# Seven half-size products for token blocks 2 and 3 in the first MLP's first matmul (slices 2 to 7)

## The chip, the core and the metric

The program runs on one core of one Trainium2 chip. The metric is device time in microseconds (us) of one execution; the number to be predicted is the median of several executions of the changed kernel. Five engines work side by side, each through its own queue in order: TensorE (PE, matmuls, with weight loads PEld that overlap them), VectorE (DVE), ScalarE (ACT), GpSimd (POOL) and SyncE (SP, which issues the transfers from HBM). Semaphores tie the queues together. A wait holds up everything that stands behind it in the same queue.

## The reference

The operator is a linear attention, a dense MLP and a domain-weighted MLP, one after the other, over 2304 tokens of width 512:

```python
def _attn_ref(q, k, v, g_norm):
    kv = np.einsum('bhsd,bhse->bhde', k, v)
    out = np.einsum('bhsd,bhde->bhse', q, kv)
    rms = np.sqrt(np.mean(out * out, axis=-1, keepdims=True) + 1e-06)
    return (out / rms * g_norm).astype(np.float32)

def _moe_ref(x, w_in, w_out):            # x 2304 x 512, w_in 512 x 2048, w_out 2048 x 512
    h = np.maximum(x @ w_in, 0.0)
    return (h * h @ w_out).astype(np.float32)

def _moe2_ref(x, domain_probs, w1, w2):  # four domains, w1 512 x 1024, w2 1024 x 512 each
    p = domain_probs / (domain_probs.sum(-1, keepdims=True) + 1e-09)
    for e in range(4):
        h = np.maximum(x @ w1[e], 0.0)
        out += p[:, e:e + 1] * (h @ w2[e])
    return out
```

The weights of the first MLP, w_in and w_out, arrive as float64; all other inputs are float32.

## The kernel before

**Numbers in two halves.** Every matmul operand is held as a high part and a low part (`split`: ACT copies the rounded high part, POOL subtracts it from the full value to get the low part). A product is three matmuls, low times high, high times low and high times high, so a 128-deep step of a product costs three matmuls of up to 512 columns.

**Tiles.** The tokens stand in five blocks (`BLK`): blocks 0 to 3 of 512 tokens, block 4 of 256. The hidden dimension of an MLP is cut into slices of 256. The first MLP has slices 0 to 7; the second MLP has 16 slices and is run in two groups, blocks 0, 1 and 4 first (slices 8 to 23 of the program), then blocks 2 and 3 (slices 24 to 39).

**Units.** The order of the work is a list of short names, each a call of one function:

- `f v.j.c` (`g1`): first product of slice v, block j, hidden half c: 4 depth steps of 3 matmuls, 12 in all, then in the first MLP ACT takes the relu, squares it and copies the high part `hh`, and POOL makes the low part `hl`.
- `g v.j.c` (`g2a`): second product of the first MLP for one 128-wide piece of the output, 6 matmuls; DVE adds the result from PSUM into the accumulator `acc`.
- `s v.b.i` (`g1s`), for i from 0 to 6: the first product of two blocks together in the second MLP, by seven products of half depth (6 matmuls of 512 columns each) in place of eight. The four PSUM banks are called pa, pb, pc and pd. Between the products run an ACT copy p1 and five DVE additions, u2, u4, and then the results of pb, pc and pd in place. Products 4, 5 and 6 add into banks pc, pa and pd that were written before, so product 4 waits for u4 to have read pc, product 5 for p1 to have read pa, and product 6 for the addition that makes pb to have read pd.
- `h` (`g2b`): second product of the second MLP. `x` (`right`): makes the sums of token blocks that `s` needs, when a group begins.
- `w` (`split_w`) takes the next 512-wide piece of weights and calls for a later one. In the first MLP a slice has four pieces, two of w_in and two of w_out; `w` starts `narrow`, five DVE operations and one ACT operation that turn float64 into two float32, and `y` (`split_narrowed`) splits the oldest narrowed piece, one operation on ACT and two on POOL. In the second MLP `w` works on pieces of two, and `operands` makes the sums of quarter tiles of the weights (four DVE operations) that `s` needs.

**Order.** `RAMP` is an order written out by hand for attention and slices 0 and 1; `rest()` makes the order after that. For slices 2 to 7 it runs over the blocks 0, 1, 2, 3, 4: first product of one block (`f` twice), second product of the block before (`g` four times), then a `y` and a `w` for the weights of a later slice. The instructions of each engine come out nearly in that order, shifted where a scheduler saw a wait. The short-lived tiles come from one pool, `tmp`, with eight places; a ninth waits until one is given back.

Of the kernel before, what the change touches and what calls it, by code (L numbers as in the profile page):

```python
# [120 lines left out]
def fused_kernel(ctx, tc, kvm, kvt, qt, g2, probs, w64, w32, out):  # L121
# [112 lines left out]

    def operands(i, v):
        r = raw.pop(i).rearrange("p c (k f) -> p (c k) f", k=2)
        w_t[v] = [
            wp.tile([P, 2, 4, 2, P], F32R, tag="a", name=f"a{v}"),  # L240
            ext.tile([P, 2, 4, 2, P], F32R, tag="a2", name=f"a2_{v}", bufs=2),
        ]
# [396 lines left out]
```

## Time and profile before

| | us |
|---|---|
| median of 3 runs | 1216.82 (1216.55 to 1217.67) |
| the profiled execution, its own time | 1214.15 |
| its span in the trace | 1212.4 |

The profiled execution is 2.67 us under the median and lies 1.75 us over its own span. Busy times of an engine are shares of the span. The matmuls of the trace overlap each other (one of 512 columns shows 390 ns, but the next begins earlier), so a rate per matmul is to be taken from a run of matmuls without a gap, not from the mean of one.

### The profile page before, as it was taken

How to read it: one execution, taken by the hardware profiler on the slowest of the kernel's cores; microseconds unless marked ns; L12 is line 12 of the kernel's file. 1: busy time of each engine (PE TensorE's matmuls, PEld its weight loads, DVE VectorE, ACT ScalarE, POOL GpSimd, SP SyncE). 2: the span in 40 equal slices, each digit the busy share in tenths (PEclk: the TensorE clock that was granted, in tenths of full speed). 3: DMA queues.
4: the chain of work that ended last, by engine and by line, in shares of the span. 5: the costliest groups of instructions: out<-in, count | busy, mean ns of one | idle time of the engine just before them, and what ended most of it. 6: DMA issues, size and time to landing. Idle time of an engine off the chain costs nothing.

```text
span 1212.4 us, 14974 instructions
## 1 busy us (share of the span) xinstructions
PE 1193.0 (98%) x5768; PEld 1003.2 (83%) x5768; DVE 765.8 (63%) x1177; ACT 439.9 (36%) x798; POOL 500.3 (41%) x390
## 2 busy tenths in 40 slices
PE   7999999999999999999999999999999999999998
PEld 6888788888888888888888888888788888888887
DVE  5968845545546466566666566656876666666655
ACT  4575444434445563222222222322433232323220
POOL 3556635445546675222323222323645242434310
PEclk9999999999999999999999999999999999999999
DMA  8611201111111101110111101111131121111101
GB/s 317 233 42 53 88 18 53 35 36 53 44 44 45 59 20 33 37 36 35 36 53 35 52 35 35 36 52 35 52 123 70 35 70 35 67 38 63 42 1 70
DMA packets 22247, 70.20 MB, mean 58 GB/s; under 512 B 2720, under 2 KB 2720, under 8 KB 22176
## 3 DMA queue, kind: packets, MB, share of 16 engines
q1 hardware_dynamic: 21888, 69.22, 16.7%
q8 instruction: 45, 0.74, 0.2%
q14 instruction: 26, 0.21, 0.1%
q10 hardware_dynamic: 288, 0.04, 0.0%
HBM read 64.52 MB, written 4.72 MB: 57 GB/s over the span
## 4 chain that ended last, share of the span: by engine, by line
PE 91%; DVE 5%; DMA 1%; issue 1%; POOL 1%; ACT 1%; SPq 0%; DVEq 0%; POOLq 0%; ACTq 0%
PE p L529 32%; PE p L377 18%; PE p L398 15%; PE pa L484 7%; PE pd L484 7%; PE pc L484 7%; PE pb L484 4%; PE po L301 1%; DVE u L179 1%; DMA kvs<-in_kvm 1%; DVE u L182 1%; DVE k L188 1%; DMA raw<-in_w 1%; DVE u L175 0%; PE pt L344 0%
## 5 line engine op out<-in xcount | busy, mean ns | idle before, releaser
L529 PE MATMUL p<-b,hh 128*128 128x512 f32 x1152 | 382.8, 390 | 0.5 <-ACT hh L516 0.5
L529 PEld LDWEIGHTS p<-b,hh 128*128 128x128 f32 x1152 | 216.3, 188 | 45.0 <-ACT hh L516 0.7
L539 DVE SCALAR_TENSOR_TENSOR acc<-p,p_sb,acc 128x512 f32<-128x512 f32 x270 | 199.4, 745 | 49.7 <-PE p L529 49.1
L529 PE MATMUL p<-b,hl 128*128 128x512 f32 x576 | 224.6, 390 | 0.0
L377 PE MATMUL p<-x,a 128*128 128x512 f32 (+1 forms) x960 | 204.3, 368 | 0.0
L377 PEld LDWEIGHTS p<-x,a 128*128 128x128 f32 x960 | 167.7, 189 | 30.4 <-PE po L301 0.2
L398 PE MATMUL p<-hh,b 128*128 128x512 f32 (+1 forms) x640 | 189.7, 370 | 0.0
L149 POOL TENSOR_TENSOR a<-raw,a 128x512 fp32r<-128x512 f32 x64 | 85.6, 1338 | 232.8 <-DVE pd L511 149.0
L405 DVE TENSOR_TENSOR acc<-p,acc 128x512 f32<-128x512 f32 (+1 forms) x140 | 87.9, 633 | 142.6 <-PE p L398 141.7
L149 POOL TENSOR_TENSOR b<-raw,b 128x512 fp32r<-128x512 f32 x64 | 82.1, 1303 | 188.0 <-ACT b L148 186.7
L149 POOL TENSOR_TENSOR hl<-s,hh 128x512 fp32r<-128x512 f32 (+1 forms) x80 | 97.9, 1226 | 120.0 <-ACT hh L148 116.7
L398 PEld LDWEIGHTS p<-hh,b 128*128 128x128 f32 x640 | 116.5, 189 | 20.2 <-ACT hh L148 0.4
L529 PEld LDWEIGHTS p<-b,hl 128*128 128x128 f32 x576 | 108.2, 188 | 21.4 <-DVE hl L517 0.2
L398 PE MATMUL p<-hl,b 128*128 128x512 f32 (+1 forms) x320 | 118.3, 370 | 2.4 <-POOL hl L149 2.4
L484 PE MATMUL pc<-o,a 128*128 128x512 f32 x384 | 97.6, 390 | 2.1 <-DVE u L499 2.1
L484 PE MATMUL pa<-o,a 128*128 128x512 f32 x384 | 97.6, 389 | 0.0
L484 PE MATMUL pd<-o,a 128*128 128x512 f32 x384 | 97.4, 389 | 0.0
L149 POOL TENSOR_TENSOR a<-w,a 128x512 fp32r<-128x512 f32 x64 | 85.0, 1328 | 25.3 <-ACT a L148 25.3
L148 ACT ACTIVATE a<-raw 128x512 fp32r<-128x512 f32 x64 | 40.1, 629 | 140.6 <-DMA raw<-in_w 109.2
L382 ACT ACTIVATE r<-p 128x512 f32<-128x512 f32 (+1 forms) x80 | 44.1, 552 | 122.2 <-PE p L377 121.7
L484 PEld LDWEIGHTS pc<-o,a 128*128 128x128 f32 x384 | 72.0, 188 | 17.5 <-DVE u L499 2.5
L484 PEld LDWEIGHTS pd<-o,a 128*128 128x128 f32 x384 | 72.1, 188 | 15.0
(92 smaller groups left out, 1477.3 us busy)
## 6 DMA issues: line engine op xcount, KB each, us to landing
raw<-in_w SPq DMA_DIRECT2D x96, 512.0 KB, 3.7
kvm<-in_kvm SPq DMA_DIRECT2D x10, 512.0 KB, 4.0
q<-in_qt SPq DMA_DIRECT2D x18, 256.0 KB, 4.6
out<-acc SPq DMA_DIRECT2D x18, 256.0 KB, 3.5
kvs<-in_kvm SPq DMA_DIRECT2D x6, 512.0 KB, 7.2
kvt<-in_kvt SPq DMA_DIRECT2D x4, 256.0 KB, 6.0
p_raw<-in_probs ACTq DMA_DIRECT2D x1, 36.0 KB, 4.8
g_sb<-in_g ACTq DMA_DIRECT2D x1, 0.5 KB, 4.3
```

The source lines that it names most:

```text
L148: nc.scalar.activation(out=hi, in_=full, func=AF.Copy)
L149: nc.gpsimd.tensor_tensor(out=lo, in0=full, in1=hi.bitcast(F32), op=ALU.subtract)
L179: nc.vector.scalar_tensor_tensor(out=u, in0=high, scalar=0xC0000000, in1=u, op0=ALU.bitwise_and, op1=ALU.bitwise_or)
L182: nc.vector.scalar_tensor_tensor(out=u.bitcast(F32), in0=k, scalar=1.125 * 2.0**-15, in1=u.bitcast(F32), op0=ALU.is_ge, op1=ALU.mult,)
L188: nc.vector.scalar_tensor_tensor(out=k.bitcast(F32), in0=low, scalar=2.0**-52, in1=k.bitcast(F32), op0=ALU.mult, op1=ALU.mult)
L377: nc.tensor.matmul(pt[:, :n], w, x, start=(i == 0), stop=(i == len(steps) - 1))
L382: nc.scalar.activation(out=r[:, :n], in_=pt[:, :n], func=AF.Relu)
L398: nc.tensor.matmul(pt[:, :n], w, h, start=(i == 0), stop=(i == len(steps) - 1))
L405: nc.vector.tensor_tensor(out=a, in0=pt[:, :n], in1=a, op=ALU.add)
L484: nc.tensor.matmul(pr[bank], x, y, start=(m == 0 and not more), stop=(m == len(steps) - 1), skip_group_check=more,)
L529: nc.tensor.matmul(pt, h, w, start=(i == 0), stop=(i == len(steps) - 1))
L539: nc.vector.scalar_tensor_tensor(out=a, in0=pt, scalar=pe, in1=a, op0=ALU.mult, op1=ALU.add)
```

## The change

In slices 2 to 7 the first product of blocks 2 and 3 is no longer four `f` units but seven `s` units, as the second MLP has them. Blocks 0, 1 and 4 stay as they are. Around it:

- The right operands (the sums t1 to t4 of the token blocks) are made once, in slice 2, by the new `right_first` (`e0` to `e3`). It writes t1, t2 and t3 into a new tile `e`, and t4 over a part of block 3's tile.
- The left operands are made for each slice: `left_parts` splits the pieces of w_in in halves of 256 columns into two tiles, a and a2, and `left_sums` adds the quarter tiles when the next `w` comes. For this `y` adds the two halves of a narrowed piece of w_in on POOL first.
- The order of the blocks in a slice is 0, 1, 4, then 2 and 3 (in slice 7: 0, 1, 2 and 3, then 4). `w` and `y` stand at other places, and `RAMP` has one `w` less, so the weights run one piece closer to their use.
- Weight tiles have two places, not three; in the second MLP a third place lies in the pool `ext`. `ext` now opens after the first MLP, so the tiles `hh` and `hl` have two places in slices 2 to 7, not three.
- `g1` squares in place of writing a second short-lived tile.

```diff
-g1.0.2 y w g0.4.3 g1.0.3 y f1.1.0 f1.1.1 f1.2.0 f1.2.1 w y w g1.1.0 g1.1.1 y g1.1.2 g1.2.0
+g1.0.2 y w g0.4.3 g1.0.3 y f1.1.0 f1.1.1 f1.2.0 f1.2.1 w y g1.1.0 g1.1.1 y g1.1.2 g1.2.0
...
-    for v in range(2, NS1):
-        for j in range(NB):
-            r += [f"f{v}.{j}.{fc}" for fc in range(FC)] + second(*prev)
-            r += ["y"] * (j > 0)
-            if j < (4, 4, 4, 4, 4, 2)[v - 2]:
-                r += ["w"]
-            prev = (v, (j,))
-            if v == NS1 - 1 and j >= 2:
-                r += [f"x0.{j - 2}"]
+    for v in range(FROM, NS1):
+        last = v == NS1 - 1
+        for n, blk in enumerate(((0,), (1,), (2, 3), (4,)) if last else ((0,), (1,), (4,), (2, 3))):
+            b = blk[0]
+            if len(blk) == 1:
+                r += [f"f{v}.{b}.{fc}" for fc in range(FC)] + second(*prev)
+                r += [f"e{n}"] if v == FROM and n < 2 else []
+                r += ["y", "w"] if n < 2 else ["y"]
+            else:
+                if v == FROM:
+                    r += ["e2", "e3"]
+                units = [f"s{v}.{b}.{i}" for i in range(7)]
+                for at, u in ((7, "x0.1"), (7, "x0.2"), (5, "x0.0")) if last else ((3, "w"),):
+                    units.insert(at, u)
+                r += merge(units[:3], second(*prev)) + units[3:] + ["y"] + ["w"] * (not last)
+            prev = (v, blk)
...
-    wp = ctx.enter_context(tc.tile_pool(name="wp", bufs=3))
+    wp = ctx.enter_context(tc.tile_pool(name="wp", bufs=2))
...
     def split_w():
+        if len(parts) == 2:
+            left_sums(parts[0][0], *(full for _, full in parts))
+            parts.clear()
...
     def split_narrowed():
         if narrowed:
-            hi, lo, top, rest = narrowed.pop(0)
+            v, c, hi, lo, top, rest = narrowed.pop(0)
+            if v >= FROM and c < 2:
+                nc.gpsimd.tensor_tensor(out=top, in0=top, in1=rest, op=ALU.add)
+                left_parts(v, c, top.rearrange("p (k f) -> p k f", k=2))
+                return
...
+    def left_parts(v, c, full):
+        for n, a in enumerate(w_t[v][:2]):
+            a = a.rearrange("p x k (h f) -> p x (k h) f", h=2)
+            split(a[:, 0, 2 * c : 2 * c + 2, :], a[:, 1, 2 * c : 2 * c + 2, :], full[:, :, n * P : (n + 1) * P])
+        parts.append((v, full))
...
+    def left_sums(v, first, other):
+        a11, a21, a12, a22 = (r[:, :, f : f + P] for r in (first, other) for f in (0, P))
+        st = [tmp.tile([P, 2, 2, P], F32, tag="tmp", name=f"w{n}_{v}") for n in range(2)]
+        s1, s2, s3, s4 = (st[n][:, m] for n in range(2) for m in range(2))
         nc.vector.tensor_tensor(out=s1, in0=a21, in1=a22, op=ALU.add)
         nc.vector.tensor_tensor(out=s2, in0=s1, in1=a11, op=ALU.subtract)
         nc.vector.tensor_tensor(out=s3, in0=a11, in1=a21, op=ALU.subtract)
         nc.vector.tensor_tensor(out=s4, in0=a12, in1=s2, op=ALU.subtract)
+        for n in range(2):
+            a = w_t[v][n].rearrange("p x k (h f) -> p x (k h) f", h=2)
+            split(a[:, 0, 4:8, :], a[:, 1, 4:8, :], st[n].rearrange("p m k f -> p (m k) f"))
...
+    def right_first(i):
+        if i == 0:
+            e = early.tile([P, 2, 6, 512], F32R, name="e")
...
+        for k in range(2):
+            full = tmp.tile([P, 512], F32, tag="tmp", name=f"{name}_{k}")
+            if name in ("t1", "t3"):
+                p, m = ("b12", "b11") if name == "t1" else ("b22", "b12")
+                low = tmp.tile([P, 512], F32, tag="tmp", name=f"{name}l_{k}")
+                nc.gpsimd.tensor_tensor(out=low, in0=half(p, k, 1), in1=half(m, k, 1), op=ALU.subtract)
+                nc.vector.tensor_tensor(out=full, in0=half(p, k, 0), in1=half(m, k, 0), op=ALU.subtract)
+            else:
+                p, m = ("b22", "t1") if name == "t2" else ("b21", "t2")
+                nc.vector.tensor_tensor(out=full, in0=half(p, k, 0), in1=t_tmp[m, k], op=ALU.subtract)
+                low = half(p, k, 1)
+            nc.vector.tensor_tensor(out=full, in0=full, in1=low, op=ALU.add)
+            split(o[:, 0, k0 + k, :], o[:, 1, k0 + k, :], full)
+            t_tmp[name, k] = full
```

How the queues change is seen at three places. The first is TensorE in slice 3, the first product of blocks 2 and 3. Before, it is four units of 12 matmuls (p1_3_2_0 is the PSUM tile of slice 3, block 2, half 0), between them second products:

```order
L377 MATMUL p1_3_2_0_2193<-x2_82,a3_1414 128x512 x12
L377 MATMUL p1_3_2_1_2212<-x2_82,a3_1414 128x512 x12
...
L377 MATMUL p1_3_3_0_2278<-x3_83,a3_1414 128x512 x12
L377 MATMUL p1_3_3_1_2297<-x3_83,a3_1414 128x512 x12
L398 MATMUL p2_3_2_0_2316<-hh3_2_2191,b3_1415 128x512
```

Now it is seven units of 6 matmuls into the banks pa to pd; between the first four stand the second products of block 4 (left out here):

```order
L554 MATMUL pa3_2_2304<-x2_82,a3_1675 128x512 x6
...
L554 MATMUL pb3_2_2321<-e_1660,a3_1675 128x512 x6
...
L554 MATMUL pc3_2_2338<-e_1660,a3_1675 128x512 x6
...
L554 MATMUL pd3_2_2383<-e_1660,a23_1676 128x512 x6
L554 MATMUL pc3_2_2338<-x3_83,a23_1676 128x512 x6
L554 MATMUL pa3_2_2304<-x2_82,a3_1675 128x512 x6
L554 MATMUL pd3_2_2383<-x3_83,a23_1676 128x512 x6
```

48 matmuls have become 42, and the last three units read and write banks that other engines have to have read first.

The second place is POOL in slice 2, between the low parts of two blocks. Before, two blocks' low parts (hl2_1, hl2_2) stand with two operations for the weights of slice 3 between them:

```order
L149 TENSOR_TENSOR hl2_1_1693<-s2_1_1_1728,hh2_1_1692 128x512
L232 TENSOR_TENSOR u3_2_1769<-u3_2_1769,b3_1415 128x512
L233 TENSOR_TENSOR b3_1415<-u3_2_1769,k3_2_1767 128x512
L149 TENSOR_TENSOR hl2_2_1778<-s2_2_0_1794,hh2_2_1777 128x512
L149 TENSOR_TENSOR hl2_2_1778<-s2_2_1_1813,hh2_2_1777 128x512
```

Now, from the second low part of block 1 on (e is the tile of t1 to t3, t3l a low difference, u3_1 the narrowed piece 1 of slice 3's weights, a3 and a23 its two tiles):

```order
L161 TENSOR_TENSOR hl2_1_1689<-r2_1_1_1721,hh2_1_1688 128x512
L161 TENSOR_TENSOR e_1660<-t2_0_1758,e_1660 128x512
L161 TENSOR_TENSOR e_1660<-t2_1_1763,e_1660 128x512
L250 TENSOR_TENSOR u3_1_1775<-u3_1_1775,k3_1_1773 128x512
L161 TENSOR_TENSOR hl2_4_1784<-r2_4_0_1798,hh2_4_1783 128x256
L524 TENSOR_TENSOR t3l_0_1859<-x3_83 128x512
L161 TENSOR_TENSOR a3_1675<-u3_1_1775,a3_1675 128x256
L524 TENSOR_TENSOR t3l_1_1866<-x3_83 128x512
L161 TENSOR_TENSOR a23_1676<-u3_1_1775,a23_1676 128x256
L161 TENSOR_TENSOR hl2_4_1784<-r2_4_1_1816,hh2_4_1783 128x256
L161 TENSOR_TENSOR e_1660<-t3_0_1858,e_1660 128x512
L161 TENSOR_TENSOR e_1660<-t3_1_1865,e_1660 128x512
```

The second low part of block 4, hl2_4, now has six new operations ahead of it (two of t2, two of t3, two weight halves) besides the sum u3_1.

The third place is DVE in slice 2, where the second products of one block are added up. Before, with pieces of the weights of slice 4 in between (p2_2_2 is the PSUM tile of the second product of block 2):

```order
L175 TENSOR_SCALAR u4_0_1941<-raw4_0_1775 128x512
L405 TENSOR_TENSOR acc1_2_989<-p2_2_2_0_1902,acc1_2_989 128x512
L179 SCALAR_TENSOR_TENSOR u4_0_1941<-raw4_0_1775,u4_0_1941 128x512
L405 TENSOR_TENSOR acc1_2_989<-p2_2_2_1_1910,acc1_2_989 128x512
L182 SCALAR_TENSOR_TENSOR u4_0_1941<-k4_0_1939,u4_0_1941 128x512
L405 TENSOR_TENSOR acc1_2_989<-p2_2_2_2_1918,acc1_2_989 128x512
```

Now, in the `s` units of slice 2 (w0 and w1 are the sums for slice 3's weights; the same twelve rows stand in slices 3 to 6, with their own numbers):

```order
L443 TENSOR_TENSOR acc1_4_1226<-p2_2_4_0_1891,acc1_4_1226 128x256
L567 TENSOR_TENSOR u2_2_2_1906<-pb2_2_1899,p1_2_2_1889 128x512
L443 TENSOR_TENSOR acc1_4_1226<-p2_2_4_1_1908,acc1_4_1226 128x256
L569 TENSOR_TENSOR u4_2_2_1923<-pc2_2_1916,u2_2_2_1906 128x512
L286 TENSOR_TENSOR w0_3_1941<-u3_0_1680,u3_1_1775 128x256
L443 TENSOR_TENSOR acc1_4_1226<-p2_2_4_2_1925,acc1_4_1226 128x256
L287 TENSOR_TENSOR w0_3_1941<-w0_3_1941,u3_0_1680 128x256
L443 TENSOR_TENSOR acc1_4_1226<-p2_2_4_3_1933,acc1_4_1226 128x256
L288 TENSOR_TENSOR w1_3_1942<-u3_0_1680 128x256
L289 TENSOR_TENSOR w1_3_1942<-u3_1_1775,w0_3_1941 128x256
L187 TENSOR_SCALAR u3_2_1953<-raw3_2_1686 128x512
L573 TENSOR_TENSOR pb2_2_1899<-pd2_2_1961,u4_2_2_1923 128x512
```

The addition that frees bank pd for product 6 stands behind the four weight sums and the first step of the next `narrow`. In slice 2 the eight DVE operations of t3 and t4 stand ahead of these rows.

## Rows read from the trace of the kernel before

**Rows 1.** The page: span, and busy time, share and instructions of each engine.
```profile
span 1212.4 us, 14974 instructions
PE 1193.0 (98%) x5768; PEld 1003.2 (83%) x5768; DVE 765.8 (63%) x1177; ACT 439.9 (36%) x798; POOL 500.3 (41%) x390
```
**Rows 2.** What TensorE waited for: us in total, times, longest.
```profile
PE pk L286 <- DMA kvs<-in_kvm: 6.1, 2, 5.0
...
PE p L398 <- POOL hl L149: 2.4, 3, 1.2
PE pc L484 <- DVE u L499: 2.1, 1, 2.1
```
**Rows 3.** Busy time by stretch: PE, PEld, DVE, ACT, POOL, clock, DMA.
```profile
250.00:300.00 50.00, 50.00 (x244) 42.35 (x243) 26.82 (x42) 22.27 (x40) 24.26 (x19) 1.00 0.14 43
300.00:350.00 50.00, 50.00 (x244) 42.35 (x243) 26.91 (x42) 21.67 (x38) 24.75 (x19) 1.00 0.13 43
850.00:900.00 50.00, 47.39 (x219) 39.18 (x218) 38.84 (x58) 21.43 (x39) 32.11 (x23) 1.00 0.32 106
```
**Rows 4.** The chain that ended last: start, length, what; slice 3, then slice 9.
```profile
212.61 5.44 PE p L377 x24
218.05 2.87 PE p L398 x24
...
261.93 5.44 PE p L377 x24
...
499.26 5.47 PE p L529 x24
...
525.30 5.47 PE p L529 x24
```
**Rows 5.** Groups, shapes apart, 250 to 450 us: busy, mean ns | idle before.
```profile
L405 DVE TENSOR_TENSOR acc<-p,acc 128x512 f32<-128x512 f32 x64 | 44.0, 688 | 72.6 <-PE p L398 72.0
L149 POOL TENSOR_TENSOR hl<-s,hh 128x512 fp32r<-128x512 f32 x32 | 43.1, 1346 | 63.3 <-ACT hh L148 62.0 <-DVE acc L405 1.4
L384 ACT ACTIVATE s<-r 128x512 f32<-128x512 f32 x32 | 20.2, 632 | 2.4
L182 DVE SCALAR_TENSOR_TENSOR u<-k,u 128x512 f32<-128x512 f32 x12 | 13.1, 1095 | 0.0
L232 POOL TENSOR_TENSOR u<-u,a 128x512 f32<-128x512 f32 x6 | 10.4, 1726 | 8.1 <-DVE k L187 6.7 <-ACT a L231 1.4
L405 DVE TENSOR_TENSOR acc<-p,acc 128x256 f32<-128x256 f32 x16 | 6.7, 421 | 22.7 <-PE p L398 22.7
L149 POOL TENSOR_TENSOR hl<-s,hh 128x256 fp32r<-128x256 f32 x8 | 5.9, 742 | 1.5 <-PE p L398 1.5
```
**Rows 6.** Single lines: duration ns min/median/max, first and last start.
```profile
L246 DVE TENSOR_TENSOR w<-raw x32: 415/426/918, 392.3 to 1139.5; 128x256 f32<-128x256 f32 x32
L247 DVE TENSOR_TENSOR w<-w,raw x32: 411/944/1529, 394.6 to 1140.3; 128x256 f32<-128x256 f32 x32
L248 DVE TENSOR_TENSOR w<-raw x32: 410/417/1528, 393.2 to 1139.9; 128x256 f32<-128x256 f32 x32
L175 DVE TENSOR_SCALAR u<-raw x32: 412/920/1526, 8.5 to 380.9; 128x512 uint32<-128x512 uint32 x32
L447 DVE TENSOR_TENSOR t<-acc,t x8: 691/1180/1777, 440.6 to 869.1; 128x512 f32<-128x512 f32 x8
```
**Rows 7.** Order of time on DVE and POOL while `x0` makes its sums.
```profile
444.94 1.78 DVE L447 TENSOR_TENSOR t<-acc,t 128x512 f32<-128x512 f32 x1
446.64 3.49 DVE L447 TENSOR_TENSOR t<-acc 128x512 f32<-128x512 f32 x2
...
446.13 3.45 POOL L438 TENSOR_TENSOR o<-t,o 128x512 fp32r<-128x512 f32 x2
```
**Rows 8.** Order of time on POOL and PE at a wait in slice 1.
```profile
134.22 1.29 POOL L149 TENSOR_TENSOR hl<-s,hh 128x512 fp32r<-128x512 f32 x1
135.47 1.28 POOL L233 TENSOR_TENSOR b<-u,k 128x512 fp32r<-128x512 f32 x1
...
138.04 0.51 PE L398 MATMUL p<-hl,b 128*128 128x512 f32 x1 [1.18 <-POOL hl L149]
```

More of the change, by code (lines that the diff above doesn't have):

```diff
@@ L63 @@
 NV = NS1 + len(GRP2) * NS2
+FROM = 2
 def slice_of(v):
@@ L71, in second @@
     if v < NS1:
-        return [f"g{v}.{j}.{c}" for j in blk for c in range(KD)]
+        return [f"g{v}.{j}.{c}" for j in blk[::-1] for c in range(KD)]
     return [f"h{v}.{j}.{t}" for j in blk[::-1] for t in range(BLK[j][1] // P)]
@@ L366, in g1, with w_of @@
         x = x_t[j]
-        hh, hl = new_h(s, j) if fc == 0 else h_t[s, j]
+        if fc == 0:
+            new_h(s, j)
         pt = ps.tile([P, 512], F32, tag="ps", name=f"p1_{s}_{j}_{fc}")
-        def left(part, k):
-            if s < NS1:
+        def w_of(part, k):
+            if s < FROM:
                 return w_t[s][0][:, part, k, fc * P : (fc + 1) * P]
-            return w_t[s][fc][:, part, k // 2, k % 2, :]
-        steps = [(left(a, k), x[:, b, k, :]) for k in range(KD) for a, b in ((1, 0), (0, 1), (0, 0))]
+            return left(s, fc, part, k // 2, k % 2)
+        steps = [(w_of(a, k), x[:, b, k, :]) for k in range(KD) for a, b in ((1, 0), (0, 1), (0, 0))]
         for i, (w, x) in enumerate(steps):
             nc.tensor.matmul(pt[:, :n], w, x, start=(i == 0), stop=(i == len(steps) - 1))
-        if s >= NS1:
-            relu(s, j, fc, pt[:, :n])
-            return
-        r = tmp.tile([P, 512], F32, tag="tmp", name=f"r{s}_{j}_{fc}")
-        nc.scalar.activation(out=r[:, :n], in_=pt[:, :n], func=AF.Relu)
-        sq = tmp.tile([P, 512], F32, tag="tmp", name=f"s{s}_{j}_{fc}")
-        nc.scalar.activation(out=sq[:, :n], in_=r[:, :n], func=AF.Square)
-        split(hh[:, fc, :n], hl[:, fc, :n], sq[:, :n])
+        hidden(s, j, fc, pt[:, :n])
     def g2a(s, j, c):
         t0, n = BLK[j]
-        b = w_t[s][1]
+        b = w_t[s][-1]
         bh, bl = b[:, 0], b[:, 1]
@@ L463, in t_sum, with half @@
         return t
+    def right_first(i):
+        if i == 0:
+            e = early.tile([P, 2, 6, 512], F32R, name="e")
+            for name, at in (("b11", (x_t[2], 0)), ("b21", (x_t[2], 2)), ("b22", (x_t[3], 2)), ("t4", (x_t[3], 0))):
+                o_t[2, name] = at
+            for n, name in enumerate(("t1", "t2", "t3")):
+                o_t[2, name] = (e, 2 * n)
+        name = ("t1", "t2", "t3", "t4")[i]
+        o, k0 = o_t[2, name]
+        def half(x, k, part):
+            t, at = o_t[2, x] if x != "b12" else (x_t[3], 0)
+            return t[:, part, at + k, :].bitcast(F32)
+        for k in range(2):
[12 more added lines that the diff above has]
+            t_tmp[name, k] = full
+        if i == 3:
+            t_tmp.clear()
     PRODUCTS = (
@@ L480, in g1s @@
         steps = [
-            (w[:, x, op, k, :], o[:, y, k0 + k, :]) for k in range(2) for x, y in ((1, 0), (0, 1), (0, 0))
+            (left(v, place, x, op, k), o[:, y, k0 + k, :]) for k in range(2) for x, y in ((1, 0), (0, 1), (0, 0))
         ]
@@ L503, in g1s, with hidden @@
             nc.vector.tensor_tensor(out=pb, in0=pd, in1=su["u4"], op=ALU.add)
[L504 removed]
+            hidden(v, j2, 1, pb)
         elif i == 4:
             nc.vector.tensor_tensor(out=pc, in0=pc, in1=su["u2"], op=ALU.add)
[L507 removed]
+            hidden(v, j2, 0, pc)
         elif i == 5:
[L509 removed]
+            hidden(v, j1, 0, pa)
         else:
             nc.vector.tensor_tensor(out=pd, in0=pd, in1=su["u2"], op=ALU.add)
[L512 to L515 removed]
+            hidden(v, j1, 1, pd)
+    def hidden(v, j, f, pt):
+        n = BLK[j][1]
+        hh, hl = (x[:, f, :n] for x in h_t[v, j])
+        if v < NS1:
+            r = tmp.tile([P, 512], F32, tag="tmp", name=f"r{v}_{j}_{f}")
+            nc.scalar.activation(out=r[:, :n], in_=pt, func=AF.Relu)
+            nc.scalar.activation(out=r[:, :n], in_=r[:, :n], func=AF.Square)
+            split(hh, hl, r[:, :n])
+            return
         nc.scalar.activation(out=hh, in_=pt, func=AF.Relu)
@@ L588, in fused_kernel @@
             run(name)
+    order = rest()
+    with tc.tile_pool(name="early", bufs=1) as early:
+        n = order.index("x0.4") + 1
+        for name in order[:n]:
+            run(name)
     ext = ctx.enter_context(tc.tile_pool(name="ext", bufs=1))
-    for name in rest():
+    for name in order[n:]:
         run(name)
```

45 lines of the change are left out of this document (23 added, 22 removed).

## The prediction

> **What bounds the kernel now.** I read the page first. TensorE is busy for 1193.0 of 1212.4 us [rows 1]; all its idle time is some 19 us. The waits of TensorE come next: the larger ones belong to the start (6.1 us for the first inputs), 2.4 us are three waits for a low part from POOL, and 2.1 us are one wait at the turn between the groups of the second MLP [rows 2]. By stretch, TensorE is busy for 50 of 50 us in the first MLP's slices [rows 3], at a clock of 1.00, while DVE has 26.8, ACT 22 and POOL 24. So in slices 2 to 7 a matmul taken away is worth its whole length, as long as nobody is late; and another engine matters only where its result comes too late for the next matmul.
>
> The length of a matmul I take from the chain: 24 of 512 columns take 5.44 us, so 0.2267 us each; 24 of 256 columns take 2.87, so 0.12 each. Slice 3 begins at 212.61 and slice 4 at 261.93: 49.32 us, which is eight pieces of 5.44 and two of 2.87 (49.26). Nothing is idle in it [rows 4]. The `s` units of the second MLP run at the same rate: slice 9 begins its second products at 499.26 and slice 10 at 525.30, 26.04 us for 102 matmuls of 512 columns and 24 of 256 (26.0) [rows 4].
>
> **The change part by part.**
>
> *Matmuls.* In each of six slices 48 matmuls become 42: 6 x 6 x 0.2267 = 8.16 us gone from TensorE. This is the whole gain.
>
> *Work added in every slice.* DVE gets five additions from PSUM (0.69 each [rows 5]) and four weight sums (0.42 when undisturbed [rows 6]): 5.1 us. ACT gets p1, two copies of sums and some shorter pieces, about 2.3 us at 0.63 [rows 5]; POOL two low parts of sums, 2.6 us at 1.3, less about 0.6 because the weight halves replace a longer step. A slice of now 47.96 us has room: in before DVE uses 26.8 of 50, POOL 24.3 [rows 3]. On average nothing binds, so what counts is the place where each result is due.
>
> *The tightest place in slices 3 to 6* is product 6, which waits for DVE's addition that makes pb. Time 0 is the start of product 0; a unit takes 6 x 0.2267 = 1.36 and a second product of block 4 0.72. Product 2 ends at 5.5, product 3 at 8.3, product 6 wants to start at 11.0. DVE's queue after product 2: u4 until 6.2, four sums of 0.42 mixed with two additions of 0.42 [rows 5, 6] until about 8.4 (the last addition's input is there at 7.0), the first narrow step 0.41 to 0.92, then pb, 0.69: done at 9.5 to 10.0. That is 1.0 us early. POOL has been idle since the low parts of block 4, so the sums should run at their 0.42. After that the chain of hidden parts: ACT has `hh` of block 3's second half at 14.8, POOL its low part at 16.1, TensorE wants it at 18.1; block 2's last low part is there at 22.9 and wanted at 24.2. Everything fits with 1 to 2 us over. For an addition late here and there I put 0.5 us for the four slices (bounds 0, and 3 if each loses 0.75). That only two places are left for `hh` and `hl` costs nothing by this walk: ACT writes block 0's `hh` when block 3's second product is through, 5.4 us before TensorE needs anything of it.
>
> *Slice 2, the sums t1 to t4.* This is the dear place. They are made once: 16 DVE operations with both operands in SBUF, eight ACT copies, and 12 POOL operations. Where DVE and POOL both work on SBUF, they hold each other up: two of each take 3.49 and 3.45 us side by side, 1.74 a pair [rows 7], against 0.69 at the least for DVE [rows 6] and 1.25 from start to start for POOL [rows 8]. So each such DVE operation adds about 0.48 to POOL. Time 0 is now the first matmul of slice 2. With no wait, product 0 would start at 27.5, the second product of block 4 at 28.9 (its fifth matmul, which reads the second low part, at 29.3), product 4 at 37.2 and product 6 at 38.5. POOL gets through the low parts of t1 and t2 by 22.5. It then needs narrowed piece 1 of slice 3's weights; DVE, with the t2 steps, five narrow steps and the accumulations, has it at 23.6. Then on POOL: the sum 24.9, block 4's first low part 25.6, t3's first difference 27.3, a weight half 28.0, the second difference 29.5, a weight half 30.2, and, with what DVE's t3 steps cost it, block 4's second low part at 31.4. TensorE loses 2.1 us there. The t4 steps on DVE wait for that same low part to give back a `tmp` place; DVE is through with t4 at 36.4, has u4 at 38.3 (product 4 is due at 37.9: 0.4 late, 0.5 with the signal), then the four sums and the narrow step, and pb at 41.5 (product 6 due at 41.1: 0.4). Sum: 3.0 us. Bounds: 1.0 if POOL and DVE disturb each other little, 7 if all 16 DVE operations take the 1.78 that is their worst [rows 6] and the chain grows by some 4 us.
>
> Here a rule of the Trainium skill speaks against the change. Its page "SBUF — State Buffer", section "SBUF: two separate sides", says that VectorE with two SBUF inputs and GpSimd share a port pair as an exclusive lock, held for a whole instruction. The trace agrees that they block each other; a lock for the whole instruction would make a pair 0.69 + 1.25 = 1.94 us, and the row has 1.74. By the rule the eight DVE steps of t3 and t4 would cost 1.6 us more, and the time would be 1214.6; the row decides for me.
>
> *From slice 7 to slice 8.* The sums for the second MLP (`x0`) now stand beside the hidden parts of blocks 2 and 3. POOL's walk from product 3 on: block 3's low part at 17.6 (due 18.1), block 2's at 23.7 (due 24.2), block 4's at 29.3 (due 29.2); DVE has its last accumulation of slice 7 a few us later than now, and p1 of slice 8 stands behind it on ACT. I put 0.8 us (0 to 2.5).
>
> *The ramp.* In slice 1 TensorE already waits 1.18 us for a low part that POOL ends at 138.0 [rows 8]. Two more POOL operations (the sums' low parts, 2.5 us) now stand ahead of it. But POOL and DVE come to them earlier: the first step on a weight piece no longer waits for an ACT copy, and DVE's last narrow step no longer meets POOL. Walked through, the low part ends between 137.4 and 138.7: no change, -0.6 to +0.7. The `w` taken out of the ramp saves nothing by itself, since it is done in slice 2.
>
> *The second MLP.* The weights are split one piece later, still a slice ahead; the queues at the turn between the groups stand as before, with the 2.1 us wait [rows 2, 3]. Nothing.
>
> Sum: -8.16 + 3.0 + 0.5 + 0.8 = -3.9 us. Against the profiled execution (1214.15) that is 1210.3; that execution lies 2.67 under the median of the runs, so I put the change on the median: 1216.82 - 3.9 = **1213.0**.
>
> **The rivals.**
>
> 1. *All hidden.* POOL orders its work in slice 2 so that nothing is late, and the margins of 1 to 2 us hold. For it: TensorE lost nothing in slices 2 to 7 so far, and the same `s` units run without a wait in slices 8 to 22 [rows 4]. Against it: there low parts of `h` come from DVE, not POOL. 1216.8 - 8.16 = 1208.7.
> 2. *Slice 2 eats the gain.* DVE's steps run near 1.78 and every later link moves with them: 7 us there and 1 to 2 at slice 8, -8.16 + 7 + 1.5 = +0.3: 1217, no change. For it: at the other place where sums are made DVE runs at a median of 1.18 and a worst of 1.78 [rows 6], and that turn is where TensorE lost 2.1 us [rows 2, 3].
> 3. *Slower: pb late in every slice.* The four sums stand ahead of pb. If POOL is at work then, they take up to 0.92, 1.53, 1.53 and 0.92, and the narrow step 1.53 [rows 6]: pb at 14.2 and not 9.5, past the 11.0 where product 6 is due. The price begins where the contention costs more than 1.0 us. Half way to the worst, pb comes at about 12.5, 1.5 us late in slices 3 to 7: 7.5 us instead of 0.5, so 1213.0 + 7 = 1220. For it: two of the sums have medians or maxima near 1 us and more. Against it: in slices 8 to 22 the same order costs nothing, and POOL should be idle there.
> 4. *The change does not do what it says*: not possible for the matmuls; the queues show 42.
>
> **How the numbers follow.** Forecast (a few us lost, most of them in slice 2): 0.45. All hidden: 0.15. Slice 2 eats the gain: 0.20. Slower: 0.15. A wait at a place not seen (ramp, turn): 0.05, of either sign. 0.2% of the time, 2.4 us, is about what the runs can tell from no change. Faster by more: 0.45 + 0.15 and little else, 0.60. Within: rival 2 and part of the last, 0.23. Slower: 0.17. The range reaches from all hidden (1208.7) to past rival 2, 1218.0; alone the forecast holds 1210.5 to 1215.5.
>
> **What would show it.** The `s` units as chains of 6 matmuls, slices of 47.96 us from 3 to 6 with no idle TensorE; in slice 2 a wait of about 2 us of a second product for a low part from POOL (block 4), then half a microsecond for u4 and for pb. Wrong would be: waits of pd units for DVE in slices 3 to 7 (rival 3), waits of over 5 us in slice 2 (rival 2), or a longer wait in the ramp than 1.2 us.

## The result and the profile after

| | before | after |
|---|---|---|
| median | 1216.92 (4 runs) | 1230.12 (1228.26 to 1234.17, 4 runs) |
| profiled execution, its own time | 1214.15 | 1229.32 |
| its span in the trace | 1212.4 | 1227.5 |

The change makes the kernel slower: ratio 1.0112, 95% interval 1.0086 to 1.0139. The forecast was 1213.0, in a range of 1208.7 to 1218.0. The page of the changed kernel, the lines that answer to [rows 1]:

```profile
span 1227.5 us, 15054 instructions
PE 1195.5 (97%) x5732; PEld 1002.3 (82%) x5732; DVE 839.8 (68%) x1247; ACT 448.5 (37%) x836; POOL 544.3 (44%) x426
```

TensorE has 36 matmuls fewer, as it should, and yet is busy for 2.5 us longer. What it waited for, as in [rows 2]:

```profile
PE p L436 <- POOL hl L161: 12.3, 8, 5.3
PE pk L330 <- DMA kvs<-in_kvm: 5.8, 2, 5.5
PE pc L554 <- DVE u L569: 3.3, 3, 2.0
```

The waits for low parts from POOL have grown from 2.4 to 12.3 us. That a shorter list of matmuls is busy for longer says that some ran slowly; the granted clock by stretch (columns as in [rows 3]) shows where:

```profile
48.00:52.00 4.00, 2.64 (x10) 2.35 (x11) 3.69 (x10) 2.86 (x6) 2.29 (x2) 0.69 0.79 281
144.00:148.00 4.00, 4.00 (x11) 3.13 (x10) 2.47 (x4) 0.63 (x1) 1.83 (x2) 0.50 0.00 0
203.00:208.00 5.00, 0.83 (x3) 0.83 (x4) 4.38 (x6) 1.26 (x2) 5.00 (x5) 0.51 0.00 0
208.00:213.00 5.00, 5.00 (x16) 4.13 (x16) 4.97 (x6) 1.12 (x2) 3.57 (x3) 0.50 0.00 0
```

The clock fell to its lower level, 1.2 GHz, in three places, each time in or just behind idle time of TensorE. In the time order of TensorE these waits are (start, length, engine, line, what; in brackets the idle time before and who ended it):

```profile
106.71 2.88 PE L422 MATMUL p<-x,a 128*128 128x512 f32 x12
...
119.89 0.50 PE L436 MATMUL p<-hl,b 128*128 128x512 f32 x1 [1.05 <-POOL hl L161]
...
140.50 0.50 PE L436 MATMUL p<-hl,b 128*128 128x512 f32 x1 [1.74 <-POOL hl L161]
...
143.41 0.80 PE L436 MATMUL p<-hl,b 128*128 128x512 f32 x1 [1.94 <-POOL hl L161]
...
207.17 0.58 PE L436 MATMUL p<-hl,b 128*128 128x256 f32 x1 [5.30 <-POOL hl L161]
...
207.76 2.76 PE L554 MATMUL pb<-e,a 128*128 128x512 f32 x6
...
470.45 0.39 PE L436 MATMUL p<-hl,b 128*128 128x256 f32 x1 [1.11 <-POOL hl L161]
...
486.69 0.50 PE L606 MATMUL p<-b,hl 128*128 128x512 f32 x1 [0.98 <-DVE hl L594]
```

**Where the time went, by stretch.** The chain that ended last gives the borders (start, length, what). Of before, in lines not needed so far, the last pieces of slice 1, then slice 7 and slice 9; the first matmul of slice 1 stands at 104.64 there, at 106.71 now:

```profile
161.83 6.90 PE p L377 x36
...
409.89 5.44 PE p L377 x24
...
485.59 1.36 PE pa L484 x6
```

Of after, the same, with the chain through the end of slice 2:

```profile
169.48 4.19 PE p L422 x24
...
218.96 0.62 DVE pb L573
219.62 1.66 PE pd L554 x6
221.28 5.44 PE p L422 x24
...
269.29 5.44 PE p L422 x24
...
413.29 5.44 PE p L422 x24
...
499.07 1.36 PE pa L554 x6
```

The first piece of each holds 1.43 us of slice 1, so slice 2 begins at 163.26 and 170.91. In the new order the second products of blocks 2 and 3 (10.88) come behind a slice's border, where before those of block 4 did (2.87); slice 2 should be 8.01 shorter by that and 1.36 by the products, and slice 7 to 9 longer by 8.01 and shorter by 1.36.

| stretch | before | after, nothing lost | after | lost |
|---|---|---|---|---|
| start to slice 1 | 104.64 | 104.64 | 106.71 | 2.1 |
| slice 1 | 58.62 | 58.62 | 64.20 | 5.6 |
| slice 2 | 49.35 | 39.98 | 50.37 | 10.4 |
| slices 3 to 6 | 197.28 | 191.84 | 192.01 | 0.2 |
| slice 7 to slice 9 | 75.70 | 82.35 | 85.78 | 3.4 |
| slice 9 to the end of the span | 726.81 | 726.81 | 728.43 | 1.6 |

23.3 lost against 8.2 gained is 15.1, the difference of the spans. So the products do give their 8 us, with 0.2 lost in slices 3 to 6. The 2.1 at the start are not the change's: a run below with the same code up to slice 2 (the sums' POOL work on DVE) begins slice 1 at 104.98. The medians differ by 13.2, which is what is left without them (13.0). The other four places, slice 1, slice 2, the turn to slice 9 and the second MLP, take back 21.0, over two and a half times the gain.

**Slice 2.** The time order of DVE there (u and k are a narrow step's, t the sums):

```profile
195.29 1.18 DVE L194 SCALAR_TENSOR_TENSOR u<-k,u 128x512 f32<-128x512 f32 x1
196.50 1.40 DVE L199 TENSOR_SCALAR k<-u 128x512 uint32<-128x512 uint32 x1
197.93 0.69 DVE L200 SCALAR_TENSOR_TENSOR k<-raw,k 128x512 f32<-128x512 uint32 x1
...
207.15 1.75 DVE L528 TENSOR_TENSOR t<-x,t 128x512 f32<-128x512 f32 x1 [0.62 <-POOL hl L161]
```

And of POOL, where t3l is a low difference and hl the low part that TensorE waits for:

```profile
194.18 3.44 POOL L161 TENSOR_TENSOR e<-t,e 128x512 fp32r<-128x512 f32 x2
198.77 1.29 POOL L250 TENSOR_TENSOR u<-u,k 128x512 f32<-128x512 f32 x1 [1.16 <-DVE k L200]
200.02 0.73 POOL L161 TENSOR_TENSOR hl<-r,hh 128x256 fp32r<-128x256 f32 x1
200.71 1.72 POOL L524 TENSOR_TENSOR t3l<-x 128x512 f32<-128x512 f32 x1
...
205.88 1.24 POOL L161 TENSOR_TENSOR hl<-r,hh 128x256 fp32r<-128x256 f32 x1
```

POOL waits for DVE's narrow step, TensorE for POOL's hl, DVE's t4 for a place that hl gives back, and product 6 at the end for pb. Every link is long while both engines work on SBUF: a narrow step takes up to 1.40, a low difference 1.72. That DVE's steps are longer because of POOL is shown by the run that takes the sums' work off POOL, below.

**Slice 1.** POOL's time order there; the two a<-w rows are the new low parts of the weight sums:

```profile
132.75 1.29 POOL L161 TENSOR_TENSOR a<-w,a 128x512 fp32r<-128x512 f32 x1
135.07 1.81 POOL L161 TENSOR_TENSOR a<-w,a 128x512 fp32r<-128x512 f32 x1 [1.02 <-ACT a L160]
...
138.99 1.45 POOL L161 TENSOR_TENSOR hl<-r,hh 128x512 fp32r<-128x512 f32 x1
```

### The profile page after: what moved, and what is told of

Read it like the earlier page. It is cut to its first block, busy times and chain, and to the rows that moved or that the text cites. A ratio compares the mean times of both kernels' runs of the same rounds, so it can differ in the third digit from the quotient of the medians.

```text
span 1227.5 us, 15054 instructions
## 1 busy us (share of the span) xinstructions
PE 1195.5 (97%) x5732; PEld 1002.3 (82%) x5732; DVE 839.8 (68%) x1247; ACT 448.5 (37%) x836; POOL 544.3 (44%) x426
## 4 chain that ended last, share of the span: by engine, by line
PE 85%; DVE 8%; POOL 3%; issue 2%; ACT 1%; DMA 1%; DVEq 0%; POOLq 0%; ACTq 0%
PE p L606 31%; PE p L436 13%; PE p L422 11%; PE pc L554 8%; PE pd L554 8%; PE pa L554 8%; PE pb L554 4%; POOL hl L161 1%; PE po L345 1%; PE pk L330 1%; DVE t L485 1%; DVE u L194 1%; DMA raw<-in_w 1%; DVE u L187 1%; DVE u L191 1%
## 5 line engine op out<-in xcount | busy, mean ns | idle before, releaser
L436 PE MATMUL p<-hh,b 128*128 128x512 f32 (+1 forms) x640 | 194.1, 375 | 0.2 <-ACT hh L160 0.2
L161 POOL TENSOR_TENSOR a<-w,a 128x512 fp32r<-128x512 f32 x76 | 102.3, 1359 | 204.9 <-DVE pd L581 125.0
L436 PEld LDWEIGHTS p<-hh,b 128*128 128x128 f32 x640 | 119.5, 192 | 21.6 <-ACT hh L160 0.7
L422 PE MATMUL p<-x,a 128*128 128x512 f32 (+1 forms) x672 | 137.0, 359 | 0.0
L436 PE MATMUL p<-hl,b 128*128 128x512 f32 (+1 forms) x320 | 120.8, 377 | 12.4 <-POOL hl L161 12.3
L422 PEld LDWEIGHTS p<-x,a 128*128 128x128 f32 x672 | 113.9, 189 | 19.5 <-PE po L345 0.2
L161 POOL TENSOR_TENSOR hl<-r,hh 128x512 fp32r<-128x512 f32 (+1 forms) x80 | 105.0, 1319 | 54.8 <-ACT hh L160 54.5
L554 PEld LDWEIGHTS pa<-o,a 128*128 128x128 f32 x384 | 72.0, 188 | 14.9
```

The lines of the kernel that those rows point to most:

```text
L161: nc.gpsimd.tensor_tensor(out=lo, in0=full, in1=hi.bitcast(F32), op=ALU.subtract)
L422: nc.tensor.matmul(pt[:, :n], w, x, start=(i == 0), stop=(i == len(steps) - 1))
L436: nc.tensor.matmul(pt[:, :n], w, h, start=(i == 0), stop=(i == len(steps) - 1))
L554: nc.tensor.matmul(pr[bank], x, y, start=(m == 0 and not more), stop=(m == len(steps) - 1), skip_group_check=more,)
```

## The experiments

The runs of before beside them have a median of 1216.91, 1216.80 and 1216.66 in the three groups (the first four runs, the next four, the last two). "Lost" is counted as in the table above, on each run's own trace. Two medians with overlapping intervals can't be told apart by their times alone; there the traces decide.

**Fill the wait of slice 2 with useless matmuls.**

```diff
+        again = 4 if (v, i) == (FROM, 0) else 0
+        for n in range(again):
+            for m, (x, y) in enumerate(steps):
+                nc.tensor.matmul(pr[bank], x, y, start=(m == 0), stop=(m == len(steps) - 1))
```

> The changed kernel, with product 0 of slice 2 (six matmuls into bank pa) done five times instead of once, the last of them as before: 24 matmuls of 512 columns more, 5.44 us of useless work, placed just ahead of the second product of block 4 that waited 5.3 us for its low part. Theory A (the wait is paid twice, once as idle time and once because the granted clock is at 0.50 behind it): the useless matmuls lie in the wait, TensorE is idle for under 1.5 us there, the clock stays at 1.00 and the time falls by about the 4.4 us that the matmuls after the wait lost, 1230.1 to about 1225.7. Theory B (the matmuls behind the wait are slow for a reason of their own, such as reading the new tile e while it is written, or the wait costs only its length): no gain, 1230 or more.

Measured: 1230.95 (ratio 1.0117, 1.0102 to 1.0132), no gain. TensorE's time order:

```profile
198.57 5.60 PE L556 MATMUL pa<-x,a 128*128 128x512 f32 x24
...
206.88 0.39 PE L436 MATMUL p<-hl,b 128*128 128x256 f32 x1 [0.88 <-POOL hl L161]
...
207.22 1.54 PE L558 MATMUL pb<-e,a 128*128 128x512 f32 x6
...
216.07 2.78 PE L558 MATMUL pc<-x,a 128*128 128x512 f32 x6 [2.38 <-DVE u L573]
```

Theory A is right on the clock: with the wait at 0.88, pb's six matmuls take 1.54 and not 2.76. It is wrong on the price. TensorE, early now, waits 2.38 for u4, and the clock falls there. The end of slice 2 is set by DVE's queue (u4, then pb), not by TensorE; at half clock it merely got there slowly. In the changed kernel pb was ready at 219.57 and product 6 began at 219.62.

**Leave out the sums of slice 2.**

```diff
-        for k in range(2):
+        for k in range(2 if i < 3 else 0):
+            for a in range(2):
+                nc.scalar.activation(out=o[:, a, k0 + k, :], in_=half("b22", k, a), func=AF.Copy)
+        for k in range(0):
```

> The changed kernel without the work for t1 to t4: DVE and POOL do none of it, ACT copies a part of block 3 into t1, t2 and t3 (12 copies in place of 8), t4's place keeps what it had. The products read wrong numbers, all else is as before. Theory A (the sums of slice 2 make POOL late for block 4's second low part, and the clock falls behind that wait): slice 2 loses under 0.5 us instead of 10.4, the ramp and the turn to slice 8 lose what they lost: 1230.1 - 10 = 1220. Theory C (the lateness in slice 2 is inherited from the ramp or comes from the weights in two places): slice 2 still loses more than 4 us, 1225 or more.

Measured: 1219.83 (ratio 1.0024, 1.0013 to 1.0036), 10.3 less than the changed kernel, 10 expected; slice 2 loses 0.1. Theory C falls for slice 2: nothing there is inherited. The wait of 5.30 is gone; the longest of TensorE's waits for POOL is now one of the ramp:

```profile
PE p L436 <- POOL hl L161: 6.6, 5, 1.9
```

**Only the second half of the change: two places, later weights.**

```diff
-FROM = 2
+FROM = 8
...
+        if v < FROM:
+            for j in range(NB):
+                r += [f"f{v}.{j}.{fc}" for fc in range(FC)] + second(*prev)
+                r += ["y"] * (j > 0)
+                if j < (2 if last else 4):
+                    r += ["w"]
+                prev = (v, (j,))
+                r += [f"x0.{j - 2}"] if last and j >= 2 else []
+            continue
```

> Only the second half of the change: no s unit in slices 2 to 7 (four f units each, blocks in the order 0 to 4), no sums, but weight tiles and hidden tiles in two places, weights one piece later, the square in place, the ramp with one w less. Theory A (all losses come from work of the products' operands on POOL and DVE): the time of the kernel before, 1216.9, within 1.5 us. Theory C (two places or the weights' later time cost TensorE waits): over 1220.

Measured: 1220.32 (ratio 1.0028, 1.0015 to 1.0040). Theory A misses, C is right: 3.4 us of the loss have nothing to do with the products. The trace has the ramp's waits at their old size (0.35 and 0.28 in place of 1.74 and 1.94; slice 1 takes 58.8 us), so the work of the left operands, halves and sums, is what is late there. New are 0.99 for hl in slice 8 and, in the turn between the groups, 1.16 and 0.40 for u4:

```profile
476.11 0.50 PE L615 MATMUL p<-b,hl 128*128 128x512 f32 x1 [0.99 <-DVE hl L603]
...
890.21 1.66 PE L563 MATMUL pc<-o,a 128*128 128x512 f32 x6 [1.16 <-DVE u L578]
907.23 1.67 PE L563 MATMUL pc<-o,a 128*128 128x512 f32 x6 [0.40 <-DVE u L578]
```

In the changed kernel, at the same places, DVE and ACT were held up in their queues by a weight transfer:

```profile
482.52 0.63 ACT L160 ACTIVATE a<-raw 128x512 fp32r<-128x512 f32 x1 [6.53 <-DMA raw<-in_w]
...
912.85 0.42 DVE L286 TENSOR_TENSOR w<-raw 128x256 f32<-128x256 f32 x1 [3.19 <-DMA raw<-in_w]
```

**From slice 3 on, the sums apart.**

The loop for slices before FROM is that of the run above, with

```diff
-FROM = 2
+FROM = 3
...
+                r += {1: ["e2"], 4: ["e0"]}.get(j, []) if v == FROM - 1 else []
...
-                r += [f"e{n}"] if v == FROM and n < 2 else []
+                r += [["e1"], ["e3"]][n] if v == FROM and n < 2 else []
...
```

> The change from slice 3 on only, slice 2 as before, and the four sums apart: t3 after block 1 of slice 2, t1 at its end, t2 and t4 after blocks 0 and 1 of slice 3. No weight sums stand in the ramp. Theory A: the ramp loses what it lost before (5.6 us less than in the changed kernel), the sums cost under 1.5 us, the gain is 5 x 1.36 = 6.8 us, the turn to slice 8 still costs about 3.4 and the turn between the groups about 1: 1216.9 - 6.8 + 4.4 + 1 = 1215.5, 1214 to 1217. Theory C (the lateness is that of the weights): the ramp is still late and the time over 1219.

Measured: 1217.44 (ratio 1.0009, 1.0000 to 1.0018), 0.4 over the range of theory A. The ramp is mended as theory A says: slice 1 takes 58.7 us. Its price for the sums misses: they still lose 3.9 in slice 3 (under 1.5 expected), where t2 and t4 stand beside the weight work of an s slice.

**The sums' POOL work on DVE.**

```diff
-                nc.gpsimd.tensor_tensor(out=low, in0=half(p, k, 1), in1=half(m, k, 1), op=ALU.subtract)
+                nc.vector.tensor_tensor(out=low, in0=half(p, k, 1), in1=half(m, k, 1), op=ALU.subtract)
...
-            split(o[:, 0, k0 + k, :], o[:, 1, k0 + k, :], full)
+            hi, lo = o[:, 0, k0 + k, :], o[:, 1, k0 + k, :]
+            nc.scalar.activation(out=hi, in_=full, func=AF.Copy)
+            nc.vector.tensor_tensor(out=lo, in0=full, in1=hi.bitcast(F32), op=ALU.subtract)
```

> The changed kernel with the twelve POOL operations of the sums t1 to t4 (four low differences, eight low parts) given to DVE, which then does 28 for the sums; all else as it was. Theory A (POOL is what makes slice 2 late: its own queue, and the steps of DVE that it stretches): with POOL at 15 operations of slice 2 in place of 27, DVE's steps run near 0.69, slice 2 loses 2 to 6 us instead of 10.4, and the time is about 1224. Theory D (DVE's queue is full in slice 2, whatever POOL does): 12 operations of 0.69 more make it later still, slice 2 loses 14 us or more, 1233 or more.

Measured: 1226.69 (ratio 1.0083, 1.0064 to 1.0102), 3.4 less than the changed kernel although DVE has twelve operations more; 6 were expected. The two intervals overlap (the changed kernel's is 1.0086 to 1.0139), but the traces show the gain: slices 2 and 3 together lose 7.6 in place of 10.4. Theory D falls. The groups of lines, shapes apart (columns as in [rows 5]), of the changed kernel, 171 to 220 us:

```profile
L530 DVE TENSOR_TENSOR t<-t,x 128x512 f32<-128x512 f32 x4 | 5.3, 1317 | 0.0
L528 DVE TENSOR_TENSOR t<-x,t 128x512 f32<-128x512 f32 x4 | 4.8, 1220 | 0.6 <-POOL hl L161 0.6
```

And of this run, 168 to 211 us:

```profile
L530 DVE TENSOR_TENSOR t<-t,x 128x512 f32<-128x512 f32 x4 | 2.7, 675 | 0.0
L528 DVE TENSOR_TENSOR t<-x,t 128x512 f32<-128x512 f32 x4 | 3.2, 802 | 0.0
```

With the sums off POOL the same steps take half and two thirds as long, and the five narrow steps of piece 1 take 3.3 us in place of 4.9. The page "Perfetto Trace Analysis" of the Trainium skill, section "Optimizing Scalar/DVE Operations", says that offloading operations between DVE and GpSimd might not help, since they share an SBUF read port. Here moving them to DVE helped, by 3.4 us: each operation is shorter on DVE (0.67 against 1.25 and more on POOL). Waits are left all the same, one of 2.49 for a low part in slice 3 among them.

This run says something of the order, too. Narrowed piece 1 came as late as in the changed kernel (27.6 us after the slice's begin, 27.7 there), and yet TensorE did not wait for block 4's second low part: POOL had made that at 193.8, ahead of its sum of the piece at 196.0. A late piece costs only what stands behind it in the queue.

**Fill the wait of slice 1.**

```diff
+        if (s, j, fc) == (1, 2, 1):
+            for i, (w, y) in enumerate(steps):
+                nc.tensor.matmul(pt[:, :n], w, y, start=(i == 0), stop=(i == len(steps) - 1))
```

> The changed kernel with one first product of slice 1 (block 2, half 1: twelve matmuls of 512 columns, 2.72 us) done twice, just ahead of the second product that waits 1.74 and 1.94 us for block 1's low parts. Behind this wait stood 5 us of matmuls at a granted clock of 0.50, and no other engine was due in them. Theory A: the useless matmuls lie in the wait, about 1 us of it is left, the clock stays at 1.00, and the time falls by the 2.6 us that the half clock cost: 1227.5. Theory B (the clock costs nothing that another engine's lateness does not take anyway, as behind the fill of slice 2): 1230 or a little more.

Measured: 1227.48 (ratio 1.0086, 1.0068 to 1.0105), 2.6 less with twelve matmuls more, as theory A had it. The intervals overlap here too; in the trace slice 1 takes 61.8 us in place of 64.2, and slice 2 is as long as it was (50.4). TensorE's time order:

```profile
143.24 0.50 PE L439 MATMUL p<-hl,b 128*128 128x512 f32 x1 [1.29 <-POOL hl L161]
```

And the granted clock, the last column but two:

```profile
144.00:148.00 4.00, 4.00 (x19) 3.29 (x19) 3.95 (x6) 0.63 (x1) 2.37 (x3) 1.00 0.00 0
```

The clock is at 1.00 from 144 to 148, where it was at 0.50. Here nobody else was due behind the wait, so the half clock had its full price; in slice 2 DVE was due.

**Two places with the weights as early as before; and from slice 3 on with them.**

```diff
-g1.0.2 y w g0.4.3 g1.0.3 y f1.1.0 f1.1.1 f1.2.0 f1.2.1 w y g1.1.0 g1.1.1 y g1.1.2 g1.2.0
+g1.0.2 y w g0.4.3 g1.0.3 y f1.1.0 f1.1.1 f1.2.0 f1.2.1 w y w g1.1.0 g1.1.1 y g1.1.2 g1.2.0
```

> The kernel without s units in slices 2 to 7 again, tiles in two places, but with the w that the change took out of the ramp put back, so that every weight piece comes as early as before. Theory E (the 3.4 us of the run without it are the later weights: at the turn to slice 8 and between the groups ACT and DVE wait in their queues for a weight transfer): back to the time of before, 1216.9 within 1 us, and no wait of slice 8's second product for hh and hl. Theory C (the two places themselves): 1219.5 or more.

> The change from slice 3 on, with the same w put back into the ramp, and the sums apart in another way: t3 after block 1, t1 after block 3 and t2 after block 4 of slice 2, t4 after block 0 of slice 3. By theory E and A: gain 5 x 1.36 = 6.8 us; the turn to slice 8 costs 1.7 (block 4's low part behind the sums of the second MLP), the sums 0.5 to 2, the later weights nothing: 1216.9 - 6.8 + 1.7 + 1.2 = 1213, 1212 to 1214.5, faster than both kernels. Theory C (two places cost): 1216 or more.

Measured: 1220.41 (ratio 1.0033, 1.0021 to 1.0045) and 1223.58 (ratio 1.0053, 1.0039 to 1.0067). Theory E is right at the turn between the groups, where only the old wait is left (2.12 and 2.13), and wrong in sum: 1216.9 and 1213 were expected, and both times lie where theory C had them (1219.5 or more, 1216 or more). With two places, early weights of the second MLP come into the way at slice 8: the first run waits 2.49 for hh, and slice 7 to slice 9 loses 5.2. In the second run that stretch loses 9.6 (1.7 expected). TensorE waits 4.03 and 1.39 us for block 2's low parts, which stand on POOL behind splits of such weights:

```profile
454.57 1.26 POOL L169 TENSOR_TENSOR a<-raw,a 128x512 fp32r<-128x512 f32 x1
455.79 1.71 POOL L169 TENSOR_TENSOR hl<-r,hh 128x512 fp32r<-128x512 f32 x1
```

The sums lose 4.7 in slices 2 and 3 of the second run (0.5 to 2 expected).

**From slice 4 on; and more w in the second MLP.**

```diff
-FROM = 2
+FROM = 4
...
+                r += {(FROM - 1, 3): ["e1"], (FROM - 1, 4): ["e3"]}.get((v, j), [])
...
+                r += {(FROM - 2, 1): ["e2"], (FROM - 1, 2): ["e0"]}.get((v, j), [])
...
-                if v == NS1 or (v - NS1) % NS2 == 0 and g:
-                    r += ["w"] * 2
+                if v == NS1:
+                    r += ["w"] * (blk == group[0])
+                elif (v - NS1) % NS2 == 0 and g:
+                    r += ["w"] * 2
+                elif v <= NS1 + 4 and blk == group[0]:
+                    r += ["w"]
```

The last lines do more than their name says. Slice 8 had four w, two behind blocks 0 and 1 and two behind block 4, and now has one; slices 9 to 12 have one more each. So three w also leave slice 8.

> The change from slice 4 on: gain 4 x 1.36 = 5.4 us. The sums are made while slices 2 and 3 still have f units (t3 after block 1 of slice 2; t1, t2 and t4 after blocks 2, 3 and 4 of slice 3), where DVE and POOL are busy for about half of the time. The weights stay one piece late in the first MLP and get one more w in each of slices 9 to 12 of the second MLP, so that they are early again at the turn between the groups. Theory F (the sums cost nothing where DVE and POOL have 20 us of 49 over; two places force the late weights, which cost only at the start and the turn of the second MLP): the sums under 1 us (3.9 in the run from slice 3 on), the turn as before (2.1 less), the ramp 0.5, the turn to slice 8 about 3.5: 1217.4 + 1.4 - 3.2 - 2.1 = 1213.5, 1212.5 to 1215, faster than the kernel before by some 0.25%. Rival G (the sums cost what they cost wherever they stand, 4 us and more): 1217 or more.

> The run from slice 3 on as it was (sums in slices 2 and 3), with the same additional w in slices 9 to 12 alone added. Theory E, for the turn alone (late weights make DVE's sums wait for a transfer there): the waits behind 885 us (1.3 and 0.6) go, 1217.4 - 2.1 = 1215.4. Theory C (the two places are what costs there): 1217.4, unchanged.

Measured: 1214.42 (ratio 0.9986, 0.9977 to 0.9996), faster than both kernels, by 0.14% against the kernel before, 0.9 over the estimate; and 1216.64 (ratio 1.0002, 0.9992 to 1.0013), 0.8 less than without the additional w, 2.1 expected. By time the second lies between theory E's 1215.4 and theory C's 1217.4 and, with overlapping intervals, decides nothing. In its trace the two waits behind 885 us are gone, as theory E has it, and slice 9 to the end takes 726.9 us in place of 728.8. The wait for hl in slice 8, 0.99 before, is 0.22 in both runs; that goes with the w that left slice 8, which no theory had in view and no run took out alone. Theory F holds, G falls: where slices 2 and 3 still have f units the sums lose 0.4 us in all. Slice 3 of the first run begins and ends in the chain at

```profile
214.73 5.44 PE p L435 x24
...
264.42 5.44 PE p L435 x24
```

which is 49.7 us, against 49.3 in [rows 4]; slice 2 loses nothing.

## Why the prediction was wrong

- *Matmuls, -8.16; slices 3 to 6, 0.5.* Right: slices of 48.0 (47.96 forecast), 0.2 lost. Rival 3, pb late in every slice, did not come. (By its own terms, six operations of 0.42 behind u4 at 6.2, DVE is through with the sums at 8.7 and not at 8.4; the margin held.)
- *Slice 2, 3.0 (1 to 7).* The place was right, and so was the order of the waits; the size was 10.4, and the leaving-out run shows that the sums are all of it. The step that failed is "DVE ... has it at 23.6", narrowed piece 1. It came at 198.62, which is 27.7 after the slice's begin, 4.1 late. The prediction lengthened POOL for each step of a sum, but gave DVE's own narrow steps no such length: undisturbed they take 0.41 to 0.69, and three of this piece's five took 1.18, 1.18 and 1.40 beside a busy POOL; steps ahead of them were stretched too (1.52 and 1.67 for the first two of piece 0); [rows 6] had a median of 0.92 for one of them. From the sum of that piece on the walk holds nearly: block 4's second low part came 7.1 us behind it (200.06 to 207.12), 6.5 were forecast. With t4's steps stretched too (6.3 us in place of 5.0), pb came at 48.7 in place of 41.5. Rival 2 had this mechanism, with 7 us for it, and a wait of over 5 us in slice 2 was its sign.
- *Ramp, 0 (-0.6 to +0.7).* Wrong, +5.6. The low part that was to end between 137.4 and 138.7 was there at 143.4; 2.1 of that is the later start of slice 1. The step that failed is that earlier steps would pay for the two low parts of weight sums ahead of it: they took 3.1 us and waited 1.0 for ACT. The waits of slice 1 grew by 3.0 (from the 2.4 of [rows 2] to 5.35, the three above and one of 0.62), and the clock behind them cost the other 2.6, which the fill of slice 1 gave back (2.6 by the medians, 2.4 in the trace).
- *Slice 7 to slice 8, 0.8 (0 to 2.5).* Wrong, 3.4: 1.1 is the wait for block 4's low part, foreseen in its place but 0.1 late in the walk; 1.4 are waits for hh and hl (0.44 and 0.98) with ACT and DVE held up by a weight transfer. The last 0.9 is not accounted for wait by wait.
- *The second MLP, nothing.* Wrong, 1.6, of which 1.2 are two new waits for u4 (0.76 and 0.47). "One piece later, still a slice ahead" was true of the weights' use, not of the queue: DVE's sums of weights stand in order ahead of u4, and waited 3.19 for the transfer ahead of the second of them. The run without any product lost 3.4 us by the weights and places alone.
- *No term for the clock.* The sum priced a wait at its length. In the ramp two waits of 3.7 us cost 6.3 with the clock behind them; in slice 2 the clock cost nothing more, since DVE was due anyway.
- *The rule of the Trainium skill on the shared port, as the prediction cites it.* It would have made the time 1214.6, still 15.5 short: the row and the rule differ by 1.6 us, less than what I left out, the stretched narrow steps (2.0 us in piece 1 alone). The row also speaks less against the rule than the prediction has it: undisturbed steps of a sum on DVE start 0.60 apart (200.25 to 202.66 in the run with the sums' POOL work on DVE, where POOL had nothing to do), which makes a pair 0.60 + 1.25 = 1.85 by the rule, against 1.74 in the row.

What stays open: with two places the weights cost some 3.5 us late and as much early; the waits were followed, but only the part at the turn between the groups, and the wait for hl in slice 8, were got rid of. And the wait of 1.1 us for block 4's low part in slice 7 stood in every version with s units there; moving the second MLP's sums away from it was not tried.

## What to carry to other kernels

A gain per slice is worth its length only if what it needs is made where the engines that make it have room: the same sums cost 10.4 us in one slice, 3.9 and 4.7 from the second block of one slice into the next, where the next had s units, and 0.4 over two slices of f units with half-idle DVE and POOL. (How far apart they stood and what stood beside them changed together, so no run shows which of the two counted.) When two engines hold each other up, lengthen the steps of both in the walk, not only of the one that is added to. Follow every piece that comes later into the queues behind it, since an in-order queue hands its wait to work that is due.

## What the runs showed of the hardware

The granted clock can fall behind the same wait in one execution and not in another. Most profiles have a wait of 1.8 to 1.9 us near 49 us; before (1.88) and the run from slice 3 on (1.88) kept 1.00 behind it, the changed kernel (1.80, the row 48.00:52.00 above) and the run without sums (1.88) did not. It costs some 1.5 us where it falls (the 2.1 of the table's first row, less 0.5 by which the first input came later, 5.5 against 5.0 in [rows 2]), and so explains a part of the scatter between executions, not all of it: in the third group of the kernel before, six executions with a mean granted clock of 0.995 took 1216.64 to 1217.24 us, and of nine with 0.999 five took 1214.46 to 1214.67, but one took 1218.27. And useless matmuls in a wait can be worth 2.6 us, if no other engine is due behind it.
